# Attention scores of two heads in the two row halves of the array, and a start-up plan that is searched

## The chip, the cores and the metric

The kernel runs on one NeuronCore of one Trainium2 chip. The metric is the device time of one execution in microseconds (us). The engines of the core work side by side, each through its own queue in order: TensorE (PE; its weight loads have a row of their own, PEld), VectorE (DVE), ScalarE (ACT), GpSimd (POOL), and SyncE (SP), which here only issues DMAs.

## What is computed

Three layers follow one another: attention over a window of 128 positions with a linear bias, a mixture of four dense experts, and one more two-layer network. Shapes: 2 batches, 8 heads, 576 positions, head dimension 64; 1152 tokens of 512 for the two networks. Cut to what matters:

```python
scores = (q @ k.T) / 8 + bias           # per batch and head; kept for 0 <= row - column < 128
attn   = softmax(scores); a = attn @ v  # (1152, 512) after the heads are joined
x = sum_e p[:, e] * (relu(a @ w1[e]) @ w2[e])     # 4 experts
h = relu(x @ w_in);  out = (h * h) @ w_out
```

Inputs are fp32. Large products are made from two rounded parts (fp32r, "high" and "rest"): a product of two numbers is high x high + high x rest + rest x high.

## The kernel before

**Stages.** All of attention, and the three first token chunks of expert 0, are laid out by a planner (class `Plan`); the trace shows this part up to about 118.6 us. After it a hand-written loop runs the other 16 or so groups of products, and background work fills the other engines. This change leaves the code of that loop alone.

**Attention in units.** A unit is one pair of heads (there are 4 pairs, `NP`). The units 0 to 3 take the first 128 rows of both batches, unrounded ("raw"): `first_load` brings q and k into partitions 0 to 63 only, and every score product is one fp32 matmul of 64 rows (L871). The 16 units after them take one batch and two row tiles each: 8 units with two full tiles (128 rows, 256 columns) and 8 with one full tile and one of 64 rows, a "twin" tile, in which two heads stand above one another in the 128 output rows. So there are 24 full tiles and 8 twin tiles.

**Scores of a full tile.** The host lays out every q twice, one copy under the other, so that `load_q` fills 128 partitions per head; `kh` rounds k into partitions 0 to 63 of `khl`, and `kl` writes its rest into partitions 64 to 127. One matmul with the rounded q over all 128 rows gives high x high and high x rest, a second with the rest of q the other two products. That makes two fp32r matmuls of 256 columns for each head, four for a tile (L879), and the same four with 192 columns for a twin tile (L863).

**After the scores** of a tile: `join` (DVE) folds the two column halves, `top` (DVE, L917) adds the bias and finds the extreme, `exp` (ACT, L926), `inv` (DVE), `norm` (POOL, ACT or DVE), `turn` (PE transposes into `tp`, L966), `hi` copies to `pt`, and POOL cuts `pt` in two. `pv` multiplies with v (L764 raw, L778): for these matmuls the output of one head goes to partitions 0 to 63 and that of the other to 64 to 127, so each has 64 weight columns, that is half of the array's columns. `evx`, `evh`, `evl` copy and round the result for the expert's first products: L1839 raw (fp32), L1051 rounded; the second products are L1790 and L1287.

**What sets the order.** Each `plan.add` names a task, the engines that may take it with modelled durations, what it depends on, the buffers that it takes and a due time. `run` picks, step by step, the engine with the earliest possible start and on it the task with the earliest due time among those that can start within 0.15 us. The instructions are emitted in that order and each engine runs its own in order; semaphores do the rest, so a model that is off makes an engine wait for a task that others could have gone before. Where the model sees PE without work in the first 24 us, `keep_busy` (L560) puts in matmuls on a tile of zeros.

The modelled PE time of a tile's scores is `us = G * (0.25 if raw else 2 * max(0.107, w * 0.00047))`, with G heads and w columns.

Of the kernel before, what the change touches and what calls it, by code (L numbers as in the profile page):

```python
# [16 lines left out]
P = 128  # L17
# [12 lines left out]
class Buf:  # L30
# [3 lines left out]
    def __init__(self, kind):  # L34
        self.kind, self.users, self.end, self.tile = kind, 0, 0.0, None


class Plan:
# [7 lines left out]
    COLD = 3.0  # L46
    WARM = 24.0
    HELD = 0.65
    SLOWED = 0.3

    def __init__(self, slots):
        self.tasks = []
        self.slots = slots
        self.held = {k: [] for k in slots}
        self.at = dict(PE=0.0, ACT=0.0, DVE=0.0, POOL=0.0, SP=0.0)
        self.port = dict(POOL=None, DVE=None)

    def add(
        self, name, opts, fn, deps=(), takes=(), bufs=(), due=0.0, follow=(), cold=True,
        shared=False  # L60
    ):
        t = dict(
            name=name, opts=opts, fn=fn, deps=[d for d in deps if d], takes=list(takes),
            bufs=list(takes) + list(bufs), due=due, end=None, follow=[d for d in follow if d],
            cold=cold, shared=shared,
        )
        for b in t["bufs"]:
            b.users += 1
        self.tasks.append(t)
        return t  # L70

    def ready(self, t):
        r = 0.0
        for d in t["deps"]:
            if d["end"] is None:
                return None
            r = max(r, d["end"] + 0.08)
        for d in t["follow"]:
            if d["end"] is None:
                return None  # L80
            r = max(r, d["start"])
        want = {}
        for b in t["takes"]:
# [3 lines left out]
            if i >= 0:  # L87
                if held[i].users:
# [4 lines left out]
    def run(self, until=None):  # L93
        todo = self.tasks
        while todo and not (until and until()):
            cand = []
            for t in todo:
# [4 lines left out]
                for eng, occ, lat in t["opts"]:  # L102
                    start = max(self.at[eng], r)
# [4 lines left out]
                cand.append((best, t))  # L108
            assert cand, [t["name"] for t in todo[:20]]
            first, _ = min(cand, key=lambda c: c[0][1])  # L110
            eng, start = first[0], first[1]
            (eng, start, occ, lat), t = min(
                (c for c in cand if c[0][0] == eng and c[0][1] <= start + self.LOOK),
                key=lambda c: c[1]["due"],
            )
            other = self.port["POOL" if eng == "DVE" else "DVE"]
            if other and (eng == "POOL" or eng == "DVE" and t["shared"]):
# [3 lines left out]
                else:  # L121
# [4 lines left out]
                    self.at["POOL"] = max(self.at["POOL"], other["start"] + other["occ"])  # L126
                occ, lat = occ + more, lat + more
            t["start"], t["end"], t["occ"] = start, start + lat, occ
            self.gap = start - self.at[eng] if start < self.WARM else 0.0
            self.at[eng] = start + occ  # L130
            if eng == "POOL" or eng == "DVE" and t["shared"]:
                self.port[eng] = t
            for b in t["takes"]:
                self.held[b.kind].append(b)
            t["fn"](eng)
            for b in t["bufs"]:
                b.users -= 1
                b.end = max(b.end, t["end"])
            todo.remove(t)
# [3 lines left out]
def kernel(  # L143
# [24 lines left out]
    NQ = 4  # L168
# [321 lines left out]
    def last_runs(nt):  # L490
# [17 lines left out]
        rq=3, rk=2, rv=4, qh=2, ql=2, khl=2, sc=2, tp=2, ts=5, st=5, pt=4, work=2, y=2, h=4  # L508
# [6 lines left out]
        sc=[actx.enter_context(tc.tile_pool(name="psc", bufs=2, space=PSUM))],  # L515
# [38 lines left out]
    def keep_busy(place):  # L554


        early = plan.at["PE"] < 1.0 and plan.gap > 2.0
        lead, each = (0.6, 0.11) if early else (-0.2, 0.08)
# [67 lines left out]

    units = [dict(bs=(0, 1), t0=0, t1=1, c=c, col=0) for c in range(NP)]
# [8 lines left out]
    task = {}  # L636

    def x_done():
        first_x.append(None)
        if len(first_x) == 1 + NP + FT:  # L640
            free.append(first_x[0][1])

    def unit_tasks(u, due):
        d = units[u]
        bs, t0, t1, c = d["bs"], d["t0"], d["t1"], d["c"]
        nb = len(bs)
        G = 2 * nb
# [3 lines left out]
        full, left = divmod(nk, P)  # L651


        raw = t0 == 0
# [7 lines left out]
        def load_q(eng):  # L662
            t = b_["rq"].tile = a_tile("rq", [P, G * nq], F32)
            blocks = [(q0, q1)] if not left else [(q0, q1 - left), (q1 - left, q1)]
            for s0, s1 in blocks:
                nc.sync.dma_start(
                    out=t[:, G * (s0 - q0):G * (s1 - q0)].rearrange("p (a s) -> p a s", a=G),
                    in_=qT[bs[0], 2 * c:2 * c + 2, :, s0:s1].rearrange("a p s -> p a s"),
                )

        def load_k(eng):
            t = b_["rk"].tile = a_tile("rk", [D, G, nk], F32)
            nc.sync.dma_start(
                out=t, in_=kT[bs[0], 2 * c:2 * c + 2, :, k0:q1].rearrange("a p s -> p a s")
# [19 lines left out]
        def qh(eng):  # L694
            b_["qh"].tile = a_tile("qh", [P, G * nq], F32R)
            rounded(eng, b_["qh"].tile, b_["rq"].tile)

        def ql(eng):
            b_["ql"].tile = a_tile("ql", [P, G * nq], F32R)
            rest(eng, b_["ql"].tile, b_["rq"].tile, b_["qh"].tile)  # L700


        def kh(eng):
            b_["khl"].tile = a_tile("khl", [P, G, nk], F32R)
            rounded(eng, b_["khl"].tile[0:D], b_["rk"].tile)

        def kl(eng):
            t = b_["khl"].tile
            rest(eng, t[D:P], b_["rk"].tile, t[0:D])
# [4 lines left out]
        if raw:  # L714
            lq, lk, lv = task["first", "q", c // 2], task["first", "k", c // 2], task["first", "v"]
        else:
            lq = add("lq", dma(2 * kbytes * nq, 1 + bool(left)), load_q, takes=[b_["rq"]], due=first - 12.0,
# [5 lines left out]
        if not raw:  # L723
            tqh = add("qh", [act(G * nq), dve(G * nq)], qh, shared=True, deps=[lq], takes=[b_["qh"]],
                      bufs=[b_["rq"]], due=first - 9.0)
            tkh = add("kh", [act(G * nk), dve(G * nk)], kh, shared=True, deps=[lk], takes=[b_["khl"]],
# [1303 lines left out]
```

## Time and profile before

| what | us |
|---|---|
| three runs | 640.82, 641.75, 641.79; median 641.75 |
| the profiled execution | 641.43, of which 639.7 from the first to the last instruction |
| PE busy | 633.3 (99%) |
| DVE, ACT, POOL busy | 470.3, 299.3, 384.3 |
| scores, L879, L863 and L871 together | some 40 of 633 by the records, which overlap |

A PE record lasts longer than it holds the engine, since matmuls are pipelined: the next one starts while the last still drains. What a matmul costs in a row of others is therefore read as the distance from its start to the start of the next (0.12 us for 256 columns), and not as its mean duration (0.28). An fp32 matmul has two records. A record's start can also be early, where it then stands and waits; the second record after a change shows when the stream really moved on.

### The profile page before, as it was taken

The page shows a single profiled execution, that of the slowest core. Times are in us where ns is not written, and L with a number is a line of the kernel's source. Part 1 is how long each engine was busy: PE and PEld are TensorE (multiplying, and loading weights), DVE is VectorE, ACT ScalarE, POOL GpSimd, SP SyncE. Part 2 cuts the span into 40 slices and gives each one's busy share as a digit, 9 for nine tenths or more (in the row PEclk, how much of TensorE's full clock was granted, in tenths as well). Part 3 has the DMA queues.
Part 4 walks back from the last instruction along what each step waited for, and adds up shares of the span by engine and source line. Part 5 has one row for each costly group of instructions (what it writes and reads, how often), then busy time and mean ns, then how long its engine had stood idle before and what let it go on. Part 6 is the DMA issues. An engine that isn't in the chain of part 4 may idle for free.

```text
span 639.7 us, 11060 instructions
## 1 busy us (share of the span) xinstructions
PE 633.3 (99%) x3929; PEld 569.2 (89%) x3929; DVE 470.3 (74%) x1023; ACT 299.3 (47%) x763; POOL 384.3 (60%) x497
## 2 busy tenths in 40 slices
PE   9999999999999999999999999999999999999997
PEld 8778899899898898998998998999999898998996
DVE  6999975378897877777777777768768767667463
ACT  6998765135354344344334334345554544343230
POOL 2589776179667447447447446346687786766531
PEclk9999999999999999999999999999999999999999
DMA  9964330222133444434434434312123223001012
GB/s 233 265 159 104 98 94 26 99 66 99 34 116 115 133 132 127 134 119 141 129 112 157 130 107 127 119 69 67 34 77 124 82 83 116 17 1 51 1 66 83
DMA packets 46983, 64.70 MB, mean 101 GB/s; under 512 B 6480, under 2 KB 29264, under 8 KB 46928
## 3 DMA queue, kind: packets, MB, share of 16 engines
q1 hardware_dynamic: 35520, 39.48, 20.9%
q10 hardware_dynamic: 11408, 24.51, 12.9%
q8 instruction: 31, 0.51, 0.3%
q14 instruction: 24, 0.20, 0.1%
HBM read 53.23 MB, written 10.75 MB: 100 GB/s over the span
## 4 chain that ended last, share of the span: by engine, by line
PE 98%; ACT 1%; DVE 0%; POOL 0%; issue 0%; POOLq 0%
PE yacc L1261 38%; PE hps L1170 35%; PE hps L1051 7%; PE yacc L1287 7%; PE xps L778 2%; PE sc L879 2%; PE tp L966 1%; PE hps L1839 1%; PE yacc L1790 1%; PE sc L560 1%; PE xtp L1353 1%; PE sc L863 1%; ACT ts L926 1%; PE sc L871 0%; PE xps L764 0%; PE ylast L1261 0%
## 5 line engine op out<-in xcount | busy, mean ns | idle before, releaser
L1261 PE MATMUL yacc<-wh,hmem 128*128 128x512 f32 x716 | 228.0, 390 | 0.0
L1261 PEld LDWEIGHTS yacc<-wh,hmem 128*128 128x128 f32 x716 | 134.6, 188 | 27.0
L1261 PE MATMUL yacc<-wl,hmem 128*128 128x512 f32 x358 | 139.9, 391 | 0.0
L536 POOL TENSOR_TENSOR wl<-wraw,wh 128x256 fp32r<-128x256 f32 (+1 forms) x79 | 74.0, 962 | 39.3 <-ACT wh L469 27.7
L536 POOL TENSOR_TENSOR hmem<-c,hmem 128x320 fp32r<-128x320 f32 (+1 forms) x64 | 59.3, 944 | 60.4 <-ACT hmem L1201 60.4
L536 POOL TENSOR_TENSOR ls<-wsum,hs 128x256 fp32r<-128x256 f32 x77 | 61.4, 825 | 54.3 <-ACT hs L414 53.6
L1185 DVE TENSOR_TENSOR u<-hps,p 128x256 f32<-128x256 f32 (+1 forms) x80 | 36.4, 455 | 65.0 <-PE hps L1170 63.1
L1181 ACT ACTIVATE p<-hps 128x256 f32<-128x256 f32 (+1 forms) x80 | 32.8, 410 | 108.8 <-PE hps L1170 108.7
L1261 PEld LDWEIGHTS yacc<-wl,hmem 128*128 128x128 f32 x358 | 67.3, 188 | 12.4
L307 DVE SCALAR_TENSOR_TENSOR wconv<-wraw,wconv 128x512 int32<-128x512 int32 x64 | 58.1, 907 | 1.3
L536 POOL TENSOR_TENSOR la<-wraw,ha 128x256 fp32r<-128x256 f32 x54 | 48.6, 919 | 16.7 <-ACT ha L400 16.7
L1205 ACT ACTIVATE hmem<-c 128x256 fp32r<-128x256 f32 (+1 forms) x72 | 31.3, 445 | 52.8 <-DVE c L1185 51.1
L1206 DVE SCALAR_TENSOR_TENSOR hmem<-c,hmem 128x256 fp32r<-128x256 f32 (+1 forms) x72 | 42.7, 614 | 14.0 <-ACT hmem L1205 13.0
L1201 ACT ACTIVATE hmem<-c 128x320 fp32r<-128x320 f32 (+1 forms) x64 | 27.3, 445 | 52.4 <-DVE c L1195 33.6
L1170 PE MATMUL hps<-ht,ls 128*128 128x320 f32 (+1 forms) x160 | 47.5, 297 | 1.3 <-POOL ls L536 1.3
L1170 PE MATMUL hps<-xh,hs 128*128 128x320 f32 (+1 forms) x160 | 47.7, 298 | 0.0
L1170 PE MATMUL hps<-ht,hs 128*128 128x320 f32 (+1 forms) x160 | 47.6, 297 | 0.0
L1170 PE MATMUL hps<-lt,hs 128*128 128x320 f32 (+1 forms) x160 | 47.4, 296 | 0.0
L1170 PE MATMUL hps<-xl,hs 128*128 128x320 f32 (+1 forms) x160 | 47.4, 296 | 0.0
L1170 PE MATMUL hps<-xh,la 128*128 128x320 f32 (+1 forms) x160 | 47.4, 296 | 0.0
L1170 PE MATMUL hps<-xl,ha 128*128 128x320 f32 (+1 forms) x160 | 47.4, 296 | 0.0
L1170 PE MATMUL hps<-xh,ls 128*128 128x320 f32 (+1 forms) x160 | 47.4, 296 | 0.0
(164 smaller groups left out, 1640.1 us busy)
## 6 DMA issues: line engine op xcount, KB each, us to landing
wraw<-in_w_dram SPq DMA_DIRECT2D x32, 512.0 KB, 3.9
wraw<-in_w_out_dram ACTq DMA_DIRECT2D x16, 512.0 KB, 3.9
w<-wconv ACTq DMA_DIRECT2D x32, 256.0 KB, 4.1
wraw<-w SPq DMA_DIRECT2D x16, 512.0 KB, 3.7
wraw<-in_w_in_dram ACTq DMA_DIRECT2D x14, 512.0 KB, 4.2
rq<-in_qT_dram SPq DMA_DIRECT2D x8, 256.0 KB, 7.7
out_dram<-y SPq DMA_DIRECT2D x7, 256.0 KB, 2.1
rk<-in_kT_dram SPq DMA_DIRECT2D x8, 192.0 KB, 5.6
```

The source lines that it names most:

```text
L307: nc.vector.scalar_tensor_tensor(out=ai, in0=raw[j][:, :, part], scalar=amount, in1=ai, op0=op, op1=ALU.bitwise_or,)
L536: e.tensor_tensor(out=out, in0=in0, in1=f32(in1), op=ALU.subtract)
L778: nc.tensor.matmul(out=xps[a * D:(a + 1) * D, x, o0:o0 + w], lhsT=held["rv"].tile[0:r, k, a * D:(a + 1) * D], rhs=held["pt"].tile[0:r, a, ...
L1051: nc.tensor.matmul(out=ps, lhsT=l_[:, k, cs], rhs=r_[:, k, cols], start=(k == 0 and r_ is xh and l_ is wh and not second), stop=(k == KT - ...
L1170: nc.tensor.matmul(out=ps, lhsT=a[l_][:, k, :], rhs=b[r_][:, k, :], start=start and k == 0 and l_ == r_, stop=stop and k == 1 and l_ == 1, ...
L1181: nc.scalar.activation(out=out, in_=x, func=ACTF.Copy)
L1185: nc.vector.tensor_tensor(out=out, in0=x, in1=y, op=ALU.add)
L1201: nc.scalar.activation(out=hh, in_=r, func=ACTF.Copy)
L1205: nc.scalar.activation(out=hh, in_=src, func=ACTF.Relu)
L1206: nc.vector.scalar_tensor_tensor(out=hl, in0=src, scalar=0.0, in1=f32(hh), op0=ALU.max, op1=ALU.subtract)
L1261: nc.tensor.matmul(out=y, lhsT=l_[:, ns], rhs=r_[:, fo, cols], start=(first and fo == 0 and j == 0), stop=(last and fo == FTQ - 1 and j == 2),
L1287: nc.tensor.matmul(out=y, lhsT=l_[:, ns], rhs=r_[:, fo, :], start=(first and j == 0), stop=(last and j == 2),)
```

## The change

Scores are computed for two heads at once: head 0 of a pair lies in partitions 0 to 63 of q and k, head 1 in 64 to 127, and the matmuls of the two heads alternate. The three rounded products are three matmuls for each head, with 64 rows each; the two heads write different banks of PSUM, and the two tiles that can be in flight share these two banks. Twin tiles and the raw units use unrounded q and k. q and k are loaded once per pair (q was loaded twice per head), and rounded with half as many elements per partition.

The planner places tasks for a given list of due times (`lay`), takes the PE waits that it sees, shifts due times near one of them at random, lays again, and keeps what does not end later by its own model, 600 times. Several modelled durations and buffer counts are others, the buffers of weights (`wb`) are now counted by the planner, and `keep_busy` has another rule.

```diff
-        lead, each = (0.6, 0.11) if early else (-0.2, 0.08)
+        lead, each = (-0.9, 0.107) if plan.gap > 3.0 else (-0.05, 0.056)
...
         def load_q(eng):
-            t = b_["rq"].tile = a_tile("rq", [P, G * nq], F32)
...
+            t = b_["rq"].tile = a_tile("rq", [P, nq], F32)
+            both = qT[bs[0], 2 * c:2 * c + 2, :, q0:q1].rearrange("a p s -> (a p) s")
+            nc.sync.dma_start(out=t, in_=both[D:D + P])
...
         def kh(eng):
-            b_["khl"].tile = a_tile("khl", [P, G, nk], F32R)
-            rounded(eng, b_["khl"].tile[0:D], b_["rk"].tile)
+            b_["khl"].tile = a_tile("khl", [P, 2, nks], F32R)
+            rounded(eng, b_["khl"].tile[:, 0, :], b_["rk"].tile[:, 0:nks])
...
         def scores(eng):
-            sc = s["sc"].tile = ps_tile("sc", [P, G, w], "sc")
+            if "banks" not in state:
+                state["banks"], state["sc"] = ps_tile("sc", [P, 2, 2, 2 * P], "sc"), 0
+            sc = s["sc"].tile = state["banks"][:, :, state["sc"] % 2, 0:w * G // 2]
...
-                qs = q_at(g, o, n)
-                for ql in (b_["qh"].tile, b_["ql"].tile):
-                    nc.tensor.matmul(
-                        out=sc[0:n, g, :], lhsT=ql[:, qs],
-                        rhs=b_["khl"].tile[:, g, j0:j0 + w],
...
+            if twin:
+                terms = [(b_["rq"].tile[:, t * P - q0:], b_["rk"].tile[:, j0:j0 + w])]
+            else:
+                qs, ks = slice(t * P - q0, t * P - q0 + n), slice(j0, j0 + w)
+                qh, ql = (b_[x].tile[:, qs] for x in ("qh", "ql"))
+                kh, kl = (b_["khl"].tile[:, x, ks] for x in range(2))
+                terms = [(qh, kh), (qh, kl), (ql, kh)]
+            for j, (q_, k_) in enumerate(terms):
+                for a in range(2):
+                    rows, o = slice(a * D, (a + 1) * D), a * n if twin else 0
                     nc.tensor.matmul(
+                        out=sc[o:o + n, a, :], lhsT=q_[rows], rhs=k_[rows], start=(j == 0),
+                        stop=(j + 1 == len(terms)), skip_group_check=True,
...
-        us = G * (0.25 if raw else 2 * max(0.107, w * 0.00047))
+        us = 0.125 * G if raw or twin else 3 * max(0.107, w * 0.00047)
...
+        for _ in range(self.ROUNDS):
+            if not waits:
+                break
+            to, _ = chance.choices(waits, [w for _, w in waits])[0]
+            trial = list(due)
+            for i, s in enumerate(starts):
+                if to - 10.0 < s < to + 3.0 and chance.random() < 0.15:
+                    trial[i] += chance.gauss(0.0, 4.0)
+            end, o, w = self.lay(trial)
+            if end is not None and end <= least:
```

What stands on PE around a full tile of scores and a product with v, the first such place before (`khl,qh` and `khl,ql` are the two matmuls of a head, 128 rows; `xps` the product with v):

```order
L1051 MATMUL hps<-xh,wl 128x256
L879 MATMUL sc<-khl,qh 128x256
L879 MATMUL sc<-khl,ql 128x256
L879 MATMUL sc<-khl,qh 128x256
L879 MATMUL sc<-khl,ql 128x256
L778 MATMUL xps<-pt,rv 64x128 x2
L778 MATMUL xps<-pt,rv 64x256 x2
L778 MATMUL xps<-pt,rv 64x128 x4
```

The same engine in the changed kernel, at a place with two full tiles (`khl,qh` x4 are high x high and high x rest for both heads, `khl,ql` x2 the third product; each has 64 rows):

```order
L1111 MATMUL hps<-xh,wl 128x256
L941 MATMUL sc<-khl,qh 128x256 x4
L941 MATMUL sc<-khl,ql 128x256 x2
L941 MATMUL sc<-khl,qh 128x256 x4
L941 MATMUL sc<-khl,ql 128x256 x2
L1026 MATMUL tp<-ident,ts 128x128 x2
```

Six matmuls of 64 rows stand where four of 128 rows stood. Of the 24 full tiles two stand among the zero matmuls of the start; the other 22 stand in 16 blocks, of which 10 have matmuls of 128 rows and 128 columns on both sides and 6 stand next to a product with v. Of the 8 twin tiles (`sc<-rk,rq 64x192 x2`) 7 stand alone and one next to such a product.

What stands at the head of ACT before (`DMAHW` would be a wait for a load, `DVE` for the extremes of L917; `ts` is the tile of a unit that the exponentials work on, four for each of the units 0 to 3):

```order
L1663 DMA first<-in_kT_dram 64x4x128 x2
L617 ACT_TABLE_LOAD
L617 ACTIVATE bias<-rel 128x128 [waits Pool_49]
L617 ACTIVATE bias<-rel 128x128 x3
L617 ACTIVATE bias<-rel 128x128 [waits DVE_49]
L617 ACTIVATE bias<-rel 128x128
L926 ACTIVATE ts,st_98<-ts,st_98 128x128 [waits DVE_49] x4
L926 ACTIVATE ts,st_99<-ts,st_99 128x128 [waits DVE_49] x4
```

And in the changed kernel:

```order
L664 ACTIVATE bias<-rel 128x128 [waits DVE_49]
L664 ACTIVATE bias<-rel 128x128
L578 ACTIVATE qh<-rq 128x256 [waits DMAHW0_49]
L578 ACTIVATE khl<-rk 128x384 [waits DMAHW1_49]
L986 ACTIVATE ts,st_98<-ts,st_98 128x128 [waits DVE_49] x4
L986 ACTIVATE ts,st_99<-ts,st_99 128x128 [waits DVE_49] x4
L986 ACTIVATE ts,st_100<-ts,st_100 128x128 [waits DVE_49] x4
L578 ACTIVATE pt<-tp 128x512 [waits PE_49]
L986 ACTIVATE ts,st_101<-ts,st_101 128x128 [waits DVE_49] x4
L578 ACTIVATE xfirst<-xps 128x256 [waits PE_49]
```

Two roundings of the first rounded unit, which wait for its loads, have moved ahead of the first exponentials, and a copy of `pt` ahead of the last four. On SP those two loads have moved ahead of the load of v.

## Rows read from the trace of the kernel before

**Rows 1.** Page, part 1: busy us, share of the span, instructions.

```profile
PE 633.3 (99%) x3929; PEld 569.2 (89%) x3929; DVE 470.3 (74%) x1023; ACT 299.3 (47%) x763; POOL 384.3 (60%) x497
```

**Rows 2.** Stretches: us; busy (instructions) by engine; clock, DMA, GB/s.

```profile
0.00:17.20 17.20, 15.70 (x159) 14.29 (x160) 11.09 (x64) 11.13 (x44) 4.59 (x17) 1.00 0.93 235
17.20:118.60 101.40, 101.36 (x768) 86.72 (x766) 80.13 (x291) 75.81 (x245) 74.31 (x121) 1.00 0.44 115
```

**Rows 3.** Waits of PE from 0 to 120 us: total, times, longest.

```profile
PE tp L966 <- ACT ts L926: 0.3, 1, 0.3
```

**Rows 4.** Groups of PE by shape: weights, operand, count | busy us, mean ns.

```profile
L879 PE MATMUL sc<-khl,qh 128*128 128x256 f32 x48 | 14.8, 331 | 0.0
...
L863 PE MATMUL sc<-khl,qh 128*128 128x192 f32 x16 | 4.3, 295 | 0.0
L871 PE MATMUL sc<-first 64*128 64x128 f32 x32 | 4.1, 279 | 0.0
```

**Rows 5.** Timeline of PE, 36.3 to 39.5: start, us, line, shapes, count.

```profile
36.38 0.28 PE L879 MATMUL sc<-khl,qh 128*128 128x256 f32 x1
36.50 0.28 PE L879 MATMUL sc<-khl,ql 128*128 128x256 f32 x1
...
36.74 0.28 PE L879 MATMUL sc<-khl,ql 128*128 128x256 f32 x1
36.95 1.96 PE L778 MATMUL xps<-pt,rv 128*64 128x128 f32 x24
38.84 0.44 PE L966 MATMUL tp<-ident,ts 128*128 128x128 f32 x2
```

**Rows 6.** Timeline of PE, a twin tile at 69.4.

```profile
69.54 0.27 PE L863 MATMUL sc<-khl,ql 128*128 128x192 f32 x1
69.65 0.28 PE L863 MATMUL sc<-khl,qh 128*128 128x192 f32 x1
```

**Rows 7.** Timeline of PE in narrow stretches around raw scores, 9.7 to 12.

```profile
9.65 0.28 PE L560 MATMUL sc<-idle 128*128 128x128 bf16 x2
...
9.86 0.48 PE L871 MATMUL sc<-first 64*128 64x128 f32 x2
...
11.63 0.27 PE L871 MATMUL sc<-first 64*128 64x128 f32 x1
...
11.84 0.44 PE L966 MATMUL tp<-ident,ts 128*128 128x128 f32 x2
```

**Rows 8.** Timeline of PE's weight loads in narrow stretches at 13.54.

```profile
13.54 0.14 PEld L764 LDWEIGHTS xps<-pt,first 128*64 128x64 f32 x2
...
13.59 0.25 PEld L764 LDWEIGHTS xps<-pt,first 128*64 128x64 f32 x4
```

**Rows 9.** Timeline of PE: the end of another product with v, 63.5 to 66.

```profile
63.54 0.28 PE L879 MATMUL sc<-khl,ql 128*128 128x256 f32 x1
...
65.64 0.39 PE L1051 MATMUL hps<-xh,wh 128*128 128x256 f32 x1
65.86 0.28 PE L1051 MATMUL hps<-xl,wh 128*128 128x256 f32 x1
```

**Rows 10.** DMA issues of 4.5 to 4.6 and of 5.1 to 5.3: KB, us to landing.

```profile
first<-in_kT_dram SPq DMA_DIRECT2D x1, 128.0 KB, 4.4
...
first<-in_v_dram SPq DMA_DIRECT2D x1, 512.0 KB, 5.6
```

**Rows 11.** Timeline of SP's queue, ACT and PE in the start.

```profile
5.19 0.60 SPq L1671 DMA_DIRECT2D first<-in_v_dram  x1
...
8.17 0.40 ACT L926 ACTIVATE ts<-ts,st 128x128 f32<-128x128 f32 x1 [3.34 <-DVE st L917]
...
14.48 0.36 ACT L530 ACTIVATE xfirst<-xps 128x256 f32<-128x256 f32 x1
...
16.10 0.83 ACT L530 ACTIVATE khl<-rk 64x768 fp32r<-64x768 f32 x1
...
17.28 0.60 PE L1839 MATMUL hps<-xfirst,wraw 128*128 128x256 f32 x2
```

More of the change, by code (lines that the diff above doesn't have):

```diff
@@ L53, in __init__ @@
         self.slots = slots
-        self.held = {k: [] for k in slots}
-        self.at = dict(PE=0.0, ACT=0.0, DVE=0.0, POOL=0.0, SP=0.0)
-        self.port = dict(POOL=None, DVE=None)
+        self.gap = 0.0
     def add(
@@ L63, in add @@
             name=name, opts=opts, fn=fn, deps=[d for d in deps if d], takes=list(takes),
-            bufs=list(takes) + list(bufs), due=due, end=None, follow=[d for d in follow if d],
-            cold=cold, shared=shared,
+            bufs=list(takes) + list(bufs), due=due, follow=[d for d in follow if d],
+            cold=cold, shared=shared, next=[],
         )
@@ L68, in add @@
             b.users += 1
+        for d in t["deps"] + t["follow"]:
+            d["next"].append(t)
         self.tasks.append(t)
@@ L91, in ready, with lay @@
         return r
[L93 to L97, printed above, removed]
+    def lay(self, due):
+        self.held = {k: [] for k in self.slots}
+        at = dict(PE=0.0, ACT=0.0, DVE=0.0, POOL=0.0, SP=0.0)
+        port = dict(POOL=None, DVE=None)
+        cand, order, waits = [], [], []
+        for i, t in enumerate(self.tasks):
+            t["due_now"], t["open"] = due[i], len(t["deps"]) + len(t["follow"])
+            for b in t["bufs"]:
+                b.left, b.end = b.users, 0.0
+            if not t["open"]:
+                cand.append(t)
+        while cand:
+            ways, first = [], None
+            for t in cand:
                 r = self.ready(t)
@@ L131, in run @@
+            order.append((t, eng, gap if start < self.WARM else 0.0))
+            at[eng] = start + occ
             if eng == "POOL" or eng == "DVE" and t["shared"]:
-                self.port[eng] = t
+                port[eng] = t
             for b in t["takes"]:
                 self.held[b.kind].append(b)
+            for b in t["bufs"]:
+                b.left -= 1
+                b.end = max(b.end, t["end"])
+            cand.remove(t)
+            for d in t["next"]:
+                d["open"] -= 1
+                if not d["open"]:
+                    cand.append(d)
@@ new lines, in lay, with run @@
+        return (at["PE"] if len(order) == len(self.tasks) else None), order, waits
+    def run(self):
+        chance = random.Random(1)
+        due = [t["due"] for t in self.tasks]
+        least, order, waits = self.lay(due)
+        assert least is not None, [t["name"] for t in self.tasks if t["open"]][:20]
+        starts = [t["start"] for t in self.tasks]
+        for _ in range(self.ROUNDS):
[8 more added lines that the diff above has]
+            if end is not None and end <= least:
+                least, order, waits, due = end, o, w, trial
+                starts = [t["start"] for t in self.tasks]
+        self.least = least
+        for t, eng, gap in order:
+            self.gap = gap if eng == "PE" else 0.0
@@ L1777, in hf @@
                 )
-        a = plan.add(f"hh{it}", [act(n), dve(n)], hf, deps=[g1_done], bufs=[wb], due=due + 1.0)
+        if f % 4 == 0:
+            h_place[f // 4] = Buf("wb")
+        place = h_place[f // 4]
+        a = plan.add(
+            f"hh{it}", [act(n), dve(n)], hf, deps=[g1_done], takes=[] if f % 4 else [place],
+            bufs=[wb], due=due + 1.0, follow=[h_first[0]] if f % 4 else [],
+        )
+        if f % 4 == 0:
+            h_first[:] = [a]
         wi = 2 * (f // FTQ) + 1
@@ L1811, in item_tasks @@
         due = T0 + T1 * ch + ITEM * f
-        us = [u for u in range(len(units)) if u // NP == ch]
+        us = [NR + (ch - 1) * NP + c for c in range(NP)]
         wi = 2 * (f // FTQ)
-        split = it < 4
-        raw = ch == 0 and f < RAW1
+        split = raw = ch == 0 and f < RAW1
         half = it % 2
```

313 lines of the change are left out of this document (160 added, 153 removed).

## The prediction

> **What bounds the kernel now.** The page comes first: PE is busy for 633 of 639.7 us, and the next engine, DVE, for 470 [rows 1]. One asks then where PE could still be idle in the part that the change touches. The stretches say: in the first 17.2 us PE has only the start to do and fills up with zero matmuls, and from 17.2 to 118.6 us it is busy for 101.36 of 101.40 us [rows 2]. Its waits in the first 120 us, beside the very first, are one of 0.3 us [rows 3]. DVE, ACT and POOL have 21 to 27 us to spare in that second stretch [rows 2]. So after the start the time of PE's own instructions is the time of the kernel, and work taken off the other engines gives nothing by itself. That covers all the halved roundings and the halved load of q: they stand beside a full PE, and 0.3 us is the most that they could free.
>
> What an instruction costs PE is read from start to start. [...]
>
> **Scores of full tiles.** Before, four matmuls at 0.12 make 0.48 us a tile; 48 of L879 with the high part of q and as many with the rest are 24 tiles [rows 4]. After, three matmuls for each of two heads make three pairs. If a pair runs at once, a tile takes 0.36 us, 0.12 less, and 22 tiles after the start give back 2.6 us.
>
> Do pairs run at once? No row has matmuls in both row halves: those of 64 rows, L871, lie all in the lower one. The nearest are the column halves of the product with v. [...] In the other direction the bound is 0.12 for every matmul, 0.72 a tile; that is a rival below.
>
> **What changing the shape of the array costs.** This is the term that decides. Raw scores (64 rows) stand between matmuls of 128 rows, and PE loses time on both sides [rows 7]. Going in: the last zero matmul begins at 9.71 (9.65 plus one step of 0.06); two records of L871 end at 10.34 together, so the second, 0.27 long, begins at 10.07. From 9.71 to 10.07 are 0.36 us where 0.06 and 0.11 were due: 0.20 lost. Going out: L871 at 11.63, and of two transposes from 11.84, 0.44 together, the second begins at 12.01: 0.38 where 0.11 and 0.11 were due, 0.16 lost. Together 0.36. [...] I take 0.37 for a block of another shape, with 0.33 and 0.40 (twice the dearer side) as its bounds, and 0.2 for a change between two such shapes; nothing but a PE that waits anyway could hide it, and after 17.2 us there is none.
>
> [...]
>
> In the changed order the 22 tiles stand in 16 blocks. Ten have plain matmuls on both sides: 10 x 0.37 = 3.7 us. Six stand beside a product with v, whose own change was paid before: 6 x 0.2 = 1.2 us. The products with v of raw units 2 and 3, one block before, are two: 0.3 us.
>
> **Twin tiles.** Before 4 x 0.11 = 0.45 us. [...] Seven stand alone, 7 x 0.37 = 2.6, one beside a product with v, 0.2. [...]
>
> PE after the start: 3.7 + 1.2 + 0.3 + 2.6 + 0.2 = 8.0 lost, 2.6 + 1.0 = 3.6 back, **4.4 us more**.
>
> **The start.** Raw scores of two units become quicker (16 records in 8 pairs), but what follows is ACT's: 16 exponentials, 0.39 us each, from 8.17 to the first copy of `xfirst` at 14.48, and PE's first product with it stands at 17.28 [rows 11]. In the changed order two roundings stand ahead of these exponentials on ACT and wait for loads of 128 and 192 KB. Those take the place on SP of v's load, issued at 5.19 [rows 11]. The load ahead of it landed at 8.9 (issued at 4.5, 4.4 us) and v's 512 KB at 10.8, 1.9 us later [rows 10], so a quarter and three eighths of that size land at about 9.4 and 10.1. The rounding of k takes 0.83 us for 768 elements [rows 11], so some 0.5 for 384: the exponentials begin at about 10.6 instead of 8.17. Queued behind: twelve exponentials (4.7, to 15.3), a copy of `pt` (0.6), four exponentials (1.6, to 17.5), the copy of `xfirst` (0.36, to 17.9). At about 18.0 PE can begin with L1839's products, 0.7 us later than before. By then it lacks one unit's transposes that the old order had done (four of 0.11, 0.4) and has done two full tiles among the zeros (2 x 0.48, 1.0): net **0.2 us more**, between -0.5 (loads 0.7 earlier) and +1.0 (the load of k as late as v's). PE's further waits then have slack: it runs behind its plan by the blocks that the plan does not count.
>
> DVE's folding of a twin tile becomes two instructions, beside a full PE: nothing. Two tiles of a head now share a bank; what a read by DVE beside a write by PE costs there no row shows. It is between nothing and one read, 0.3 us, on some tiles; I take nothing, since no wait of PE on DVE shows in rows 3, and leave it to the upper end.
>
> **The sum.** 641.43 of the profiled execution + 4.4 + 0.2 = **646.0**. The median of the three runs, 641.75, is 0.3 above that execution, well inside the range.
>
> **The rivals.**
> *Faster, row halves need no drain.* If only the column shape pays and a 64-row block joins the stream for nothing, 3.6 us come back and 0.5 (products with v, start) stay: 638.3. [...] The point that decides is a price of 0.15 a block (3.6 less 0.5 over some 20 blocks); below it the change is faster.
> *It does not do what it says, halves run one after another.* [...] Against it: the column halves load side by side [rows 8].
> [...]
> *The start falls further behind.* Gaps of PE that the plan did not fill, or the shared banks, cost 2 to 3 us more: 648.5. For it: the loads land about 2.5 us later than ACT's order needs them. Against it: PE has 16 products of 0.4 us queued from about 18 us on.
>
> **How the numbers follow.** Forecast (drain paid, pairs at once) 0.62; no drain 0.18; one after another 0.10; the late start 0.10. The likeliest gives 646.0, by itself 643.5 to 648. The range goes down to the first rival and up to the third, 637.5 to 649; the serial halves are left out. A measurement tells 0.2%, 1.3 us, from no change. Faster than that: the first rival and a trace of the forecast, 0.19. Within it: a drain at half its price or a start 2 us better, 0.12. Slower: 0.69.
>
> **What would show it.** In the changed trace the records of the two heads should start some 0.01 us apart and pairs 0.12; around a block some 0.2 on each side should be lost; the first exponential should begin between 10 and 10.6 us, L1839 at about 18, and the planned part should end near 123 us instead of 118.6, with the rest shifted and no longer. Pairs 0.24 apart would make the second rival right. A second record 0.12 behind the first on the way out, with nothing lost, the first.

## The result, and the profile of the changed kernel

The changed kernel takes 647.36 us (median of four runs, 646.72 to 647.98) against 641.70 for the kernel before: 1.0091 times as long, 95% interval 1.0074 to 1.0109. It is slower, by 5.7 us; the forecast was 646.0, between 637.5 and 649.0. Where the mean granted clock of a run is 0.994 to 0.997 instead of 1.00, it takes some 1 to 2 us more (few_idle 646.72 at 1.00, 647.41 to 648.38 below; diag_joined 644.7 and 645.0 at 1.00, 646.60 to 646.96 below); what is read from traces goes by executions at 1.00 (0.999 at the least), unless it says otherwise.

The page's busy times (part 1), and its stretches (us; busy us and instructions of PE, its weight loads, DVE, ACT and POOL; clock, DMA share, GB/s), the second up to the last product with v:

```profile
PE 636.0 (99%) x4002; PEld 563.8 (87%) x4002; DVE 461.5 (72%) x1031; ACT 292.0 (45%) x761; POOL 369.3 (57%) x495
0.00:17.20 17.20, 13.23 (x173) 11.93 (x173) 9.61 (x61) 10.28 (x42) 4.57 (x17) 1.00 0.90 272
17.20:123.80 106.60, 106.39 (x816) 83.90 (x811) 73.25 (x302) 69.47 (x244) 59.44 (x119) 1.00 0.29 86
```

DVE, ACT and POOL do 7 to 15 us less than in [rows 1], and behind the start that buys nothing: PE is as full as it was in [rows 2]. In the start, though, it is busy for 13.2 of 17.2 us, where it was for 15.7. Its waits up to 126 us (engine, line and operation, what it waited for, us, times, longest):

```profile
PE sc L607 <- DVE st L976: 2.9, 2, 1.9
...
PE sc L941 <- DVE st L976: 0.2, 1, 0.2
```

The first line is new against [rows 3]. Two marks divide the loss: the first product of L1908 (L1839 before), which ends the start, and the first product of the part that is not planned, L1230 (L1170 before). The timeline of PE, before and then after:

```profile
152.60 0.28 PE L1170 MATMUL hps<-xh,ha 128*128 128x256 f32 x1
```

```profile
18.77 0.48 PE L1908 MATMUL hps<-xfirst,wraw 128*128 128x256 f32 x1
157.89 0.28 PE L1230 MATMUL hps<-xh,ha 128*128 128x256 f32 x1
```

The start ends at 18.77 instead of 17.28 [rows 11], 1.49 later. From there to the second mark PE needs 139.12 us instead of 135.32, 3.80 more. Together 5.3, and that is all: the spans are 645.0 and 639.7, so everything behind is shifted and no longer.

**A block of pairs.** The timeline of PE around two score tiles in a row, after:

```profile
26.93 0.38 PE L1026 MATMUL tp<-ident,ts 128*128 128x128 f32 x2
27.24 0.50 PE L941 MATMUL sc<-khl,qh 64*128 64x256 f32 x4
27.58 0.28 PE L941 MATMUL sc<-khl,ql 64*128 64x256 f32 x2
27.70 0.40 PE L941 MATMUL sc<-khl,qh 64*128 64x256 f32 x4
27.94 0.28 PE L941 MATMUL sc<-khl,ql 64*128 64x256 f32 x2
28.15 0.70 PE L1908 MATMUL hps<-xfirst,wraw 128*128 128x256 f32 x2
```

The pairs run at once: two records fill 0.28 us, as one does, and pairs follow at 0.12 (27.58, 27.70). The block itself is lost time at both ends. The second transpose begins at 27.04 (26.93 + 0.11), the first pair at 27.24 where 0.11 were due; the last pair begins at 27.94, the next product at 28.15, and the one behind it at 28.47 (28.85 less 0.38) where 0.12 and 0.22 were due. From 27.04 to 28.47 are 1.43 us for 0.11 + 6 x 0.12 + 0.22: 0.4 lost.

**Twin tiles**, in opposite quarters, in the same timeline:

```profile
71.28 0.38 PE L1026 MATMUL tp<-ident,ts 128*128 128x128 f32 x2
71.58 0.54 PE L941 MATMUL sc<-rk,rq 64*64 64x192 f32 x4
72.06 0.39 PE L1111 MATMUL hps<-xh,wh 128*128 128x256 f32 x1
72.28 0.28 PE L1111 MATMUL hps<-xl,wh 128*128 128x256 f32 x1
```

Four records in 0.54 us: at once too (a single product of this kind, two records, will show 0.49 below, and hold PE for 0.32). From 71.39 to 72.28 are 0.89 us for 0.11 + 0.32 + 0.12, 0.34 lost.

### The profile page after: what moved, and what is told of

It is laid out like the page before. It is cut to its first block, busy times and chain, and to the rows that moved or that the text cites. A ratio compares the mean times of both kernels' runs of the same rounds, so it can differ in the third digit from the quotient of the medians.

```text
span 645.0 us, 11186 instructions
## 1 busy us (share of the span) xinstructions
PE 636.0 (99%) x4002; PEld 563.8 (87%) x4002; DVE 461.5 (72%) x1031; ACT 292.0 (45%) x761; POOL 369.3 (57%) x495
## 4 chain that ended last, share of the span: by engine, by line
PE 91%; POOL 5%; issue 3%; DVE 1%; ACT 0%; POOLq 0%; DVEq 0%
PE yacc L1321 34%; PE hps L1230 31%; PE hps L1111 7%; PE yacc L1347 7%; PE sc L941 2%; POOL hmem L584 2%; PE xps L827 2%; PE tp L1026 1%; PE hps L1908 1%; PE yacc L1867 1%; PE sc L607 1%; POOL wsum L438 1%; PE xtp L1413 1%; POOL ls L584 1%; POOL la L584 1%
## 5 line engine op out<-in xcount | busy, mean ns | idle before, releaser
L584 POOL TENSOR_TENSOR wl<-wraw,wh 128x256 fp32r<-128x256 f32 (+1 forms) x82 | 77.7, 973 | 40.7 <-ACT wh L517 27.8
L1230 PE MATMUL hps<-ht,ls 128*128 128x320 f32 (+1 forms) x160 | 47.5, 297 | 1.2 <-POOL ls L584 1.2
L1230 PE MATMUL hps<-xh,hs 128*128 128x320 f32 (+1 forms) x160 | 47.6, 297 | 0.0
L1230 PE MATMUL hps<-ht,hs 128*128 128x320 f32 (+1 forms) x160 | 47.5, 297 | 0.0
L1230 PE MATMUL hps<-xl,hs 128*128 128x320 f32 (+1 forms) x160 | 47.4, 296 | 0.0
L1230 PE MATMUL hps<-xh,la 128*128 128x320 f32 (+1 forms) x160 | 47.4, 296 | 0.0
L1230 PE MATMUL hps<-lt,hs 128*128 128x320 f32 (+1 forms) x160 | 47.4, 296 | 0.0
L1230 PE MATMUL hps<-xl,ha 128*128 128x320 f32 (+1 forms) x160 | 47.3, 296 | 0.0
L1230 PE MATMUL hps<-xh,ls 128*128 128x320 f32 (+1 forms) x160 | 47.3, 296 | 0.0
```

Of the source, the lines that this page charges most:

```text
L584: e.tensor_tensor(out=out, in0=in0, in1=f32(in1), op=ALU.subtract)
L1230: nc.tensor.matmul(out=ps, lhsT=a[l_][:, k, :], rhs=b[r_][:, k, :], start=start and k == 0 and l_ == r_, stop=stop and k == 1 and l_ == 1, ...
```

## The experiments

### What a change of shape costs, by itself

Two kernels add one zero product at each of 80 places to the kernel before, one of 64 rows and one of 128. A third, read from its trace only, goes through four shapes.

```diff
+    def zeros(ps):
+        nc.tensor.matmul(
+            out=ps[:, 0:P], lhsT=idle[0:D], rhs=idle[0:D], start=False, stop=False,
+            skip_group_check=True,
+        )
...
+                if l_ is wh and r_ is xl and ch < 3:
+                    zeros(ps)
```

In the second kernel both operands are `idle`, all 128 rows.

> The kernel before, with one product of a zero matrix, 64 rows by 128 columns, added behind the second product of each k step in the planned part (80 places, all between fp32r products of 128 rows with PE full); it adds zeros. **Change of shape costs**: 80 x (0.06 for the product + 0.38 for the way in and out) = 35 us more, 677 us. **A block of 64 rows joins the stream for nothing**: 80 x 0.06 = 4.8 us more, 646.5 us.

> The control: the same 80 places, but the zero matrix has 128 rows, the shape of its neighbours. Both theories: 80 times one step of 0.06 to 0.12 us, 646.5 to 651 us. The difference to the kernel with 64 rows is the price of the shape alone: 30 us by the theory, 0 by the rival.

> The kernel before with zero products in the same 80 places, by turns of four shapes: 128 rows by 64 columns, 64 by 64, 64 by 128 followed at once by 128 by 64, and 64 by 128. Read from the trace only: by the theory each single one costs alike, 0.35 us from the neighbour before to the second neighbour behind beyond their own steps, and the one with two shapes in a row 0.2 more than a single one. By a rival in which it is the weight load of columns that is late, the 64 by 128 block is cheaper than 128 by 64.

Measured: 668.92 us with 64 rows (1.0431, 1.0413 to 1.0449), 650.25 with 128 (1.0140, 1.0123 to 1.0158), against 641.14 before. So a place costs 0.35 us with 64 rows and 0.11 with 128; the shape alone is 0.23, 18.7 us in all. Both theories had a wrong number: it is far from nothing, and not the 0.38 that I had put on top of the product. The timeline of PE, 64 rows first, then 128:

```profile
33.73 0.28 PE L1057 MATMUL hps<-xl,wh 128*128 128x256 f32 x1
33.94 0.23 PE L1044 MATMUL hps<-idle 64*128 64x128 bf16 x1
34.10 0.39 PE L1057 MATMUL hps<-xh,wl 128*128 128x256 f32 x1
34.32 0.28 PE L1057 MATMUL hps<-xh,wh 128*128 128x256 f32 x1
```

```profile
33.39 0.28 PE L1057 MATMUL hps<-xl,wh 128*128 128x256 f32 x1
33.51 0.23 PE L1044 MATMUL hps<-idle 128*128 128x128 bf16 x1
33.55 0.36 PE L1057 MATMUL hps<-xh,wl 128*128 128x256 f32 x1
33.75 0.28 PE L1057 MATMUL hps<-xh,wh 128*128 128x256 f32 x1
```

With 128 rows the zero product itself costs 0.04 and the product behind it 0.20 instead of 0.12; why that one takes longer, no row here shows. With 64 rows the way in costs 0.21 instead of 0.12 and the way out 0.16 and then 0.22. So a short plain product pays 0.11 of the 0.35 too; what a block costs against plain products of its own length, plain_twins below shows. The four shapes of the third kernel (timeline of PE):

```profile
33.77 0.28 PE L1066 MATMUL hps<-xl,wh 128*128 128x256 f32 x1
33.97 0.24 PE L1048 MATMUL hps<-idle 128*64 128x128 bf16 x1
...
34.37 0.28 PE L1066 MATMUL hps<-xh,wh 128*128 128x256 f32 x1
34.49 0.28 PE L1066 MATMUL hps<-xl,wh 128*128 128x256 f32 x1
34.70 0.24 PE L1048 MATMUL hps<-idle 64*64 64x128 bf16 x1
...
35.09 0.28 PE L1066 MATMUL hps<-xh,wh 128*128 128x256 f32 x1
35.20 0.28 PE L1066 MATMUL hps<-xl,wh 128*128 128x256 f32 x1
35.42 0.23 PE L1048 MATMUL hps<-idle 64*128 64x128 bf16 x1
35.57 0.24 PE L1053 MATMUL hps<-idle 128*64 128x128 bf16 x1
...
35.97 0.28 PE L1066 MATMUL hps<-xh,wh 128*128 128x256 f32 x1
```

From the neighbour before to the second one behind: 0.60 us for columns (33.77 to 34.37), 0.60 for quarters (34.49 to 35.09), 0.59 for rows (33.73 to 34.32 above), 0.77 for rows and then columns; 0.24 without a block (two steps of 0.12). One price for all three shapes, and 0.16 to 0.17 more for a second shape behind the first.

### The same plan with plain shapes

```diff
-                terms = [(qh, kh), (qh, kl), (ql, kh)]
+                terms = [(qh, kh), (ql, kl)]
+                for j, (q_, k_) in enumerate(terms):
+                    for a in range(2):
+                        nc.tensor.matmul(
+                            out=sc[0:n, a, :], lhsT=q_, rhs=k_, start=(j == 0), stop=(j == 1),
...
```

> The changed kernel, but each full tile is scored by four products of 128 rows (two a head, of the rounded q and k as they lie) instead of three pairs of 64 rows. It computes sums over both heads, so its scores are not the reference's; the order of the work, the roundings, the loads and everything else stay. **The change of shape is what costs** (my theory): 22 tiles take 22 x 0.12 = 2.6 us more than as pairs, and the losses around them go (ten blocks of about 0.4 and six of 0.2, 5.2 us): 2.6 us faster than the changed kernel, some 644.5 us, and 0.12 us from product to product. **The loss came from the plan or the start** (rival): nothing comes back and the tiles cost 2.6 us more, some 650 us.

Measured: 645.78 us (1.0073, 1.0060 to 1.0086), 1.6 below the changed kernel where 2.6 were expected. But the kernel before took 641.14 beside it, 0.6 less than beside the changed kernel; against their own kernels before, the two are 1.0 apart, and by the trace L1230's counterpart stands at 156.75, 1.14 earlier. The direction is that of the shape theory, and the rival's 650 is out, though the two intervals overlap. Where some of the rest is, two rows of PE show:

```profile
31.61 0.47 PE L940 MATMUL sc<-khl,ql 128*128 128x256 f32 x2 [0.16 <-DVE khl L584]
...
54.56 0.50 PE L940 MATMUL sc<-khl,qh 128*128 128x256 f32 x2 [0.16 <-DVE st L983]
```

At the first PE waits for a part of k that DVE rounds, at the second, and once more at a twin tile, until DVE has read the tile before: 0.7 us in all where it was 0.2. The two traces have the same order, so they can be laid side by side, product by product. Four of the 16 blocks, at 31.6, 54.6, 73.3 and 97.3 us, give back -0.1 us together where the expectation has 0.9. That is 1.0 of the 1.5 missing; two of the four are the waits shown, at the other two the cause is open. The lower price beside a product with v (0.16 for 0.2, six times) is another 0.2.

```diff
-                terms = [(b_["rq"].tile[:, t * P - q0:], b_["rk"].tile[:, j0:j0 + w])]
+                nc.tensor.matmul(
+                    out=sc[:, 0, :], lhsT=b_["rq"].tile[:, nq - P:nq],
+                    rhs=b_["rk"].tile[:, j0:j0 + w], start=True, stop=True, skip_group_check=True,
+                )
+                return
```

> The changed kernel, but a twin tile is scored by one fp32 product of 128 rows and 128 weight columns, not by two in opposite quarters of the array. Its scores of the twin tiles are not the reference's. [...] **Change of shape costs**: seven blocks of quarters stand alone and lost 0.34 each, one 0.2: 2.6 us faster than the changed kernel, 644.7 us. **Quarters cost nothing by themselves** (rival): no difference, 647.3 us.

Measured: median 647.00 (1.0079, 1.0066 to 1.0093), but four of its six runs are at a clock of 0.996 or 0.997; the two at 0.999 take 644.7 and 644.9, and the profiled one of these has its second mark at 155.94, 1.95 earlier than the changed kernel; 0.12 of that is a quicker start. With this one product in place of two the timeline of PE reads:

```profile
71.22 0.38 PE L1030 MATMUL tp<-ident,ts 128*128 128x128 f32 x2
71.43 0.49 PE L932 MATMUL sc<-rk,rq 128*128 128x192 f32 x2
...
71.88 0.28 PE L1115 MATMUL hps<-xl,wh 128*128 128x256 f32 x1
```

From 71.33 to 71.88 are 0.55 us, where the quarters took 0.89; less 0.11 and 0.12 that leaves 0.32 for the product. So the whole price of a block, 0.34, goes with its shape. Eight times 0.34 are 2.7; PE waits 0.6 for DVE where it waited 0.2, which leaves 2.3 of them, and 1.8 came between the marks. The median doesn't show it, so this rests on the trace.

Where the price arises, the weight loads tell. The timeline of PEld at this tile, first in the changed kernel, then here:

```profile
71.58 0.19 PEld L941 LDWEIGHTS sc<-rk,rq 64*64 64x64 f32 x4 [0.17 <-issue]
```

```profile
71.33 0.30 PEld L932 LDWEIGHTS sc<-rk,rq 128*128 128x128 f32 x2
```

In plain shape the first load begins together with the last transpose (71.33), 0.10 ahead of its product (71.43). With quarters it begins 0.20 behind the last transpose (71.39), together with its own product (71.58), and on the way out it is the same (72.06 for both): at these changes of shape nothing is loaded ahead.

### The plan

```diff
-    ROUNDS = 600
+    ROUNDS = 0
```

> The changed kernel with the plan as its rules lay it first, without the 600 trials of the search. By the program order it has 87 changes of shape on PE where the changed kernel has 75, and 146 zero products instead of 120. **Shape theory**: 12 changes at 0.19 us are 2.3 us more, 649.5 us, and more where PE waits in the start. **The search is what costs** (rival): faster than 647.

Measured: 653.78 us (1.0183, 1.0168 to 1.0198), 4 us worse than the count of changes gives. In the profiled execution the granted clock of the first 17.2 us was 0.90, and between 17.2 and 60 us PE was busy for 41.1 of 42.8. The search is worth 6.4 us to this kernel; at 0.19 a change, the count of shapes is 2.3 of that.

The next one keeps the changed planner and start and takes back the scores (q loaded and rounded twice, k's parts stacked, two products of 128 rows a head, L879 and L863 as they were). With them come back the smaller buffer counts (`rq` 3 for 4, `rk` 2 for 4, `qh`, `ql`, `khl` 2 for 3); the shared score banks stay, and the search finds another order:

> The searched plan, the first loads, the raw scores and all else of the change, but full and twin tiles scored as before: q loaded and rounded twice over, k's two parts stacked, two products of 128 rows a head. **Shape theory**: from L1908's counterpart on PE does what it did before, the 8 us of shape changes are gone and only a later start of 0 to 1.5 us is left: 641.5 to 643 us. **The searched plan loses by itself** (rival): 645 us or more.

Measured: 650.49 us (1.0132, 1.0113 to 1.0151). My theory missed by 8 us. It has 28 changes of shape by its records, and is slower than the kernel with 75. In its trace, an execution at 0.997, PE is busy for 40.57 of the 42.80 us from 17.2 to 60. Of its waits behind 18.7 us, 1.9 are of scores for DVE's reads and 1.0 of transposes for POOL. So the run does not undo one thing. Whether the doubled rounding, the fewer buffers, the shared banks or the order makes PE wait it can't tell, and it says nothing of the shapes; what the searched plan is worth with the old scores stays open.

```diff
+                    elif eng == "PE" and t["shape"] != shape:
+                        occ, lat = occ + self.SHAPE, lat + self.SHAPE      # 0.19
...
-                key=lambda w: w[1]["due_now"],
+                key=lambda w: w[1]["due_now"] - (
+                    self.STAY if w[0][0] == "PE" and w[1]["shape"] == shape > 0 else 0.0),
```

> The changed kernel with a plan that counts 0.19 us for each change of shape on PE, prefers by 1 us of due time to stay in a shape, and searches 2500 trials, half of them around places drawn evenly. Its program order has 57 changes of shape where the changed kernel has 75. **Shape theory**: 18 x 0.19 = 3.4 us less, 643.9 us. **The number of changes is not what matters** (rival): 647.3 us.

Measured: 646.29 us (1.0079, 1.0066 to 1.0091), 1.1 less, not 3.4, and hardly apart from the changed kernel. The profiled execution is one at 0.997, the lower clock lying in its start (0.90 in the first 17.2 us), so its time is not compared; its waits behind the start are those of its order:

```profile
PE sc L951 <- DVE st L979: 2.6, 3, 1.1
...
```

Tiles that stand side by side need the score banks sooner than DVE clears them; the changed kernel waited for 0.2 us there. From mark to mark PE needs 139.80 us, 0.7 more than in the changed kernel, so nothing of the 3.4 is to be seen there. The waits, 3.0 us more in all, are most of that by count; the search also drew other random numbers here, so the order differs in more than its shapes, and the rest has no cause on record.

### The start

```diff
-    WARM = 24.0
+    WARM = 9.5
```

> The changed kernel without the 53 zero products that the plan puts into the gaps of PE behind 9.5 us of its own clock (the first 67 stay; the order of the rest is the same). **The late start is PE's own** (theory): PE reached its first transposes at 14.07 us, when their operand had been there since 12.88, because 27 zero products and a tile stood ahead of them; without the zeros they begin at about 12.9, the first copy of xfirst and L1908's first product about 1 us earlier (17.8 instead of 18.77), the whole kernel 0.7 to 1 us faster, some 646.5 us. **ACT's queue sets it** (my prediction): nothing moves, 647.3 us. PE's clock could also fall in the gaps; then the stretch from 12 to 18 us shows a lower granted clock and the kernel is no faster.

Measured: 647.74 us (1.0095, 1.0078 to 1.0113), no gain; but three of the four runs are at 0.994 to 0.997, and the profiled one, at 1.00, takes 646.72, as the changed kernel does at its best. There the raw scores began 1.0 us later than in the changed kernel (6.18 us, 5.17), and L1908 yet 0.26 earlier. Both have the same 47 zero products ahead of the raw scores. They end between 5.0 and 6.2 us in the profiled executions of the changed kernel and its variants, with more or fewer of them 0.107 us apart (the first 19 of the changed kernel, in 2.21 us) instead of 0.055 (its 16 from 8.21 on, in 1.05 us, below). So a gain or loss of 1 us in the start can't be told by one execution, and this run leaves the theory of PE's own zeros open. My prediction's ACT it does not bear out: even here ACT idles for 1.0 us before the exponentials of the third tile, until DVE has read it. In the changed kernel the exponentials begin earlier than forecast, and later ACT's queue stands and waits for PE, in the timeline of ACT:

```profile
9.44 0.39 ACT L986 ACTIVATE ts<-ts,st 128x128 f32<-128x128 f32 x1
...
17.47 0.38 ACT L578 ACTIVATE xfirst<-xps 128x256 f32<-128x256 f32 x1 [0.62 <-PE xps L813]
```

The timeline of PE in the changed kernel, with two rows of DVE between (the first is the fourth and last read of the first tile), shows who waits for whom:

```profile
5.17 1.16 PE L926 MATMUL sc<-first 64*128 64x128 f32 x16
7.02 0.28 DVE L976 CUSTOM_DVE_ANT_0 ts<-sc,bias 128x128 f32<-128x128 f32 x1
8.21 1.05 PE L607 MATMUL sc<-idle 128*128 128x128 bf16 x16 [1.88 <-DVE st L976]
9.20 0.72 PE L926 MATMUL sc<-first 64*128 64x128 f32 x8
10.17 0.71 PE L926 MATMUL sc<-first 64*128 64x128 f32 x8
10.93 0.29 DVE L976 CUSTOM_DVE_ANT_0 ts<-sc,bias 128x128 f32<-128x128 f32 x1 [0.81 <-PE sc L926]
11.92 1.00 PE L607 MATMUL sc<-idle 128*128 128x128 bf16 x15 [1.03 <-DVE st L976]
```

PE writes two raw tiles, then waits until DVE has read both; it writes the third (to 9.9) and the fourth (to 10.9), and DVE, free for the third since 10.1, waits until the fourth is written too; then PE waits for DVE again. From 10.93 to 11.85 DVE reads one of the two; the other it reads from 13.51, when PE has written the first full tile. Each tile lies in both score banks, a head in each, and two tiles share the two. So the banks are handed to and fro as a whole. The test lays the third and fourth tile elsewhere, with the program otherwise the same:

```diff
             sc = s["sc"].tile = state["banks"][:, :, state["sc"] % 2, 0:w * G // 2]
             state["sc"] += 1
+            if u in (2, 3):
+                sc = s["sc"].tile = Halves(
+                    [ps_tile(("work", "y")[u - 2], [P, 2 * P], "scw") for _ in range(2)]
+                )
```

> The changed kernel, but the raw scores of the third and the fourth unit lie in PSUM banks of their own (those of work and y, which nothing else uses yet) instead of sharing the two score banks with the first two; the order of the program is the same. **The shared banks delay the start** (theory): PE waits for all eight of DVE's first reads before it writes the third unit, at 8.21 us, and its first full tile waits until 11.92 for reads of the third and fourth; without that L1908 begins 0.8 us earlier, about 18.0, and the kernel takes 0.8 us less, 646.5 us. **The banks don't matter** (rival, my prediction's 'nothing'): L1908 stays at 18.5 to 18.8 and the time at 647.3.

Measured: 644.83 us (1.0053, 1.0040 to 1.0067), 2.5 less than the changed kernel; the intervals do not touch. Its waits, the first raw scores and the two marks in the timeline:

```profile
...
PE sc L954 <- DVE st L989: 0.2, 1, 0.2
```

```profile
5.75 1.16 PE L939 MATMUL sc<-first 64*128 64x128 f32 x16
...
16.49 0.48 PE L1921 MATMUL hps<-xfirst,wraw 128*128 128x256 f32 x1
...
155.67 0.28 PE L1243 MATMUL hps<-xh,ha 128*128 128x256 f32 x1
```

The 2.9 us of waits are gone, L1908's counterpart begins 2.28 earlier, and the second mark 2.22. From mark to mark are 139.18 us, as in the changed kernel: this is the start alone. The raw scores of the kernel before, in its timeline:

```profile
6.61 2.08 PE L871 MATMUL sc<-first 64*128 64x128 f32 x16
```

From the first raw score to the first mark the kernel before takes 10.67 us, the changed kernel 13.60 and this one 10.73. So the shared banks cost 2.9 us of the start, all that it lost on this way. Only 1.49 of them show at the first mark, because the raw scores began 1.4 us earlier in that execution than in the one of the kernel before. The first tile, whose columns the third takes, was read by 7.30 us, and PE came back at 8.21, when the second had been read too. What the trace shows is a wait for a semaphore; what the bank itself would do without it no run tries.

### A version that is faster than both

The last two score a twin tile with one plain fp32 product. The weights are a zeroed 128 by 128 tile in which one head's 64 queries fill the upper left block and the other's the lower right one, so that one product over the 128 rows of two heads' keys gives each head the scores of its own rows. In diag_joined, which also counts changes of shape in its plan, the keys come from rk; in diag_twins, the kernel before with this change alone, from a tile of their own.

```diff
+            for a in range(2 if left else 0):
+                rows = slice(a * D, (a + 1) * D)
...
+                    out=q_twin[u % 4][rows, a * left:(a + 1) * left],
+                    in_=qT[bs[0], 2 * c + a, rows, q1 - left:q1],
...
-                            out=sc[:, g, :], lhsT=ql[:, G * o:G * (o + n)],
...
+                    out=sc[:, 0, :], lhsT=q_twin[u % 4], rhs=k_twin[u % 4], start=True, stop=True
```

> The changed kernel with both: the plan that counts changes of shape (2000 trials) and twin tiles scored by the one product with queries on the diagonal. Its order has 53 changes of shape. **Shape theory**: 22 x 0.19 = 4.2 us less than the changed kernel, 643.1 us. **Rival** (number of changes doesn't matter): 646 to 647 us.

Measured: 646.60 us (1.0069, 1.0056 to 1.0082), 0.8 less than the changed kernel; three of five runs are at 0.996 or 0.997, the other two, at 1.00, take 644.7 and 645.0, some 2 less. The profiled one of these has its first mark 0.98 earlier than the changed kernel and needs 138.62 us to the second, 0.50 less, not 4.2. Part of what the saved changes give comes back as waits, here 1.4 us behind the start; the rest isn't settled.

> The kernel before with one change: a twin tile is scored by one fp32 product of 128 rows, with the two heads' queries on the diagonal blocks of a zeroed weight tile (two heads at once, plain shape), instead of four products of 0.11 us; its q and k are not rounded. **Shape theory**: 0.33 us for 0.45, eight times, 1.0 us faster than before: 640.7 us, and no product around it loses anything. **Rival**: PE's time is not the bound there and nothing moves, 641.7.

Measured: 640.04 us against 641.61 (0.9975, 0.9966 to 0.9984): faster than both kernels. The row of PE at the second mark:

```profile
151.51 0.28 PE L1179 MATMUL hps<-xh,ha 128*128 128x256 f32 x1
```

The mark stands 1.09 us earlier than 152.60, which is the 1.0 expected; the median gives 1.6, and what the other 0.5 is no trace shows.

## Why the prediction was right, and where it was off

**The bound** held. PE is full behind the start (106.39 of 106.60 us), and less work on the other engines moved nothing there in the changed kernel. That is true of this order only: plan_only, in another, has 2.2 us of idle PE.

**Pairs at once** held, which no row of the kernel before shows for row halves: two heads' records fill 0.28 us together, pairs follow at 0.12; the quarters too (four records in 0.54 us). The rival of halves one after another is out.

**The price of a block** held in size: 0.37 was taken, with 0.33 as its lower bound. Neither stands in a row, where the raw scores lose 0.36 [rows 7]; a block of two tiles cost 0.4 (27.04 to 28.47), one of quarters 0.34. A change between two shapes was taken at 0.2 and is 0.16 to 0.17. The first rival, a block of 64 rows for nothing, is out by zeros_rows: from the product before to the second one behind are 0.59 us with 64 rows (0.60 with columns and with quarters) and 0.36 with a plain product. The prediction calls this price a drain; that the engine drains there no run shows. What the prediction did not see is where the price arises: in the blocks read, the first weights behind a change are not loaded ahead (loads from 27.24, 28.14, 71.58 and 72.06 us, their products from 27.24, 28.15, 71.58 and 72.06).

**PE's sum** held. No row shows its 1.0 us back from twin tiles; plain_twins shows 0.32 us for one product of this kind, where four products of 0.11 stood [rows 6], and diag_twins, with that product in plain shape, has its second mark 1.09 earlier. Of the 4.6 us, 3.9 lay behind L1908's first product (4.4, less two tiles at 0.48 done earlier, plus four transposes at 0.11 done later) and 0.7 in the start. Measured: 3.80 and 1.49. Of the 3.80, the two runs that take the shapes from full and from twin tiles give back 1.2 and 1.8 between the marks, each by itself.

**The start** is the step that failed, in size and in mechanism. I took ACT's queue for the chain: loads, two roundings, exponentials from 10.6 us. They began at 9.44. The loads that ACT's roundings waited for had landed by 9.01, not at 10.1, and later ACT waited for PE. The chain was that of PE and DVE over two shared banks. The prediction met that question and put it at nothing, because no wait of PE on DVE stood in [rows 3]; but those rows are of a kernel in which each tile has its own bank, so they could not show it. Its third rival named the shared banks, at 2 to 3 us, and got one chance in ten. own_banks prices them: 2.3 us by the marks, 2.5 by the medians, 2.9 from the first raw score on.

That the total still came out within 1.4 us of 646.0 is luck in part. The banks, put at nothing, cost 2.3 or more; the delay of 0.7 by ACT's queue, which was counted, did not come, and the raw scores began earlier. own_banks' L1921 stands at 16.49, 0.8 ahead of the kernel before, and so do its first raw scores (5.75, 6.61), with 47 zero products ahead of them for 51. Whether smaller loads or paired raw scores have a part in that, no run separates.

With banks of their own the change is still 3.2 us slower than before (644.83, 641.61). That the shapes cause this rest is shown by their price in the zeros, by the two blocks read above and by the runs that put plain products in place of the blocks. Those moved it the right way but by less than expected; new waits of PE for DVE explain a part of that, and the rest is open. What the searched order by itself adds or saves, no run isolates.

## What to carry to other kernels

A block of another array shape cost PE 0.34 to 0.4 us in the places read here, with PE full, whichever shape it was: count blocks, not products, and take the shape only where a block saves more than that, or set it beside one that pays already. Two heads at once can also be had in plain shape, with zeros in the weights, where a block diagonal costs no more columns (diag_twins, 640.04 us against 641.61). Before two tiles share a PSUM bank, ask who reads the one while the other is written, which cost 2.3 to 2.9 us of the start here: the traces of a kernel with a bank for each can't tell. And before a difference of 1 us in the start is given a cause, look when the first work of the start began: it moved by as much from execution to execution.

## What was not expected of the hardware

Rows, columns and quarters cost the same on the way in and out, 0.59 to 0.60 us from the product before to the second one behind, and a second shape behind the first only 0.16 to 0.17 more. And the clock: in the changed kernel's start PE waited for 1.88 us and then did 16 zero products in 1.05 us (above); in joined, behind the same wait of 1.88 us, the same 16 took 1.86, as its timeline of PE shows:

```profile
8.93 1.86 PE L617 MATMUL sc<-idle 128*128 128x128 bf16 x16 [1.88 <-DVE st L986]
```

Its granted clock was 0.90 in the first 17.2 us, the changed kernel's 1.00. What decides between the two no run shows. But the sharing of banks seems to have a second price in it: eight kernels here have that wait, and 18 of their 37 runs have a mean clock of 0.994 to 0.997; own_banks, diag_twins, the kernels with zeros and the kernel before, all without it, have none below 0.999.
